# Raw loads of q and k queued quarter by quarter, and the first pair's second-head masks put later

## The chip, the cores and the metric

The kernel runs on one core of a Trainium2 chip. The metric is the device time of one execution in microseconds (us), the median of several runs. TensorE (PE) does the matrix products, VectorE (DVE), ScalarE (ACT) and GpSimd (POOL) the elementwise work, and SyncE (SP) issues nearly all DMAs, one after another, on one queue.

## The reference

Three layers follow each other. The first is attention in clusters: every query and every key is assigned to one of 16 centroids of its head, and a query sees only the keys of its own cluster. Two layers over 1536 tokens come behind it: a dense one with a SiLU, and one that sends each token to one of eight experts.

```python
q_assign = np.argmax(np.einsum('bhsd,hcd->bhsc', q_n, c_n), axis=-1)
k_assign = np.argmax(np.einsum('bhsd,hcd->bhsc', k_n, c_n), axis=-1)
mask = q_assign[:, :, :, None] == k_assign[:, :, None, :]
scores = np.where(mask, scale * np.matmul(q, k.transpose(0, 1, 3, 2)), -1e9)
attn = softmax(scores) ; out = np.matmul(attn, v)      # B, H, S, D = 2, 8, 768, 64
x = out as [1536, 512] ; h = x @ w_in ; x = (h * sigmoid(h)) @ w_out
logits = x @ w_gate + modality_bias[modality_id] ; e = argmax(logits)
out = max(softmax(logits)) * (relu(x @ w1[e]) @ w2[e])
```

## The kernel before

Attention works on eight pairs of heads, one pair after another. For each pair the raw q, k and v come from memory (`load`), are turned into operands for the score product (`prep`), and then run through twelve chunks of 128 queries (`chunk_ops`).

The operands of a pair lie in one tile `opn`, of which there are two, `opn_0` for even pairs and `opn_1` for odd ones. It has four parts, QQ, K1, QX and KX. A score product of a chunk is two kinds of matmul: QQ by K1 (L578), and QX by KX (L581), both added in a bank `big`; there are two such banks. Three steps lead to the operands:

- **Raw loads.** v is one DMA of 384 KB (L347). q and k of pair 0 are two DMAs each (L351). q and k of the later pairs are loaded blocked, in four DMAs each, one for a quarter of the partitions (L356), and DVE transposes them in blocks of 32 (L411).
- **Moves.** ACT and POOL write halves of QQ, K1, KX and a tile `lq`; SP copies them into the other halves of the partitions (L474).
- **Masks.** A chain of seven steps on DVE and PE (L488 to L508) finds every query's and key's cluster and leaves it in `clu_0oq`; POOL makes `clu_0ok` of it (L514). For pair 0 ACT and DVE copy both into rows 64 to 95 of QX and KX (L542, L546), four copies each: two heads by two halves of the tokens. For the other pairs four DMAs do that (L538): two from `clu_0oq` into QX, two from `clu_0ok` into KX.

Then each chunk has its score product, its row maximum on DVE (`nm`, L600), its exponential on ACT (`p`, L606), six transposes on PE (`t`, L617) with their copies to `pt` on ACT (L202) or DVE (L205); every third chunk also sends the reciprocals of its row sums through memory (`rsc` L667, `rb` L672), and a product with v follows (L680). Pair 0 runs head 0 for six chunks, then head 1. Beside it the weights of the later layers begin to be loaded, the gate weights, modality ids and biases (L822 to L825) among them.

No order is written out. Every piece of work is an `op` with a guessed duration, a priority (`prio`, a lower number goes first), the pieces it depends on and the tiles it takes, and `Sched.run` plays them through, at each step taking for each engine the best that can start. What it finds is the order of the instructions on each engine; each engine then runs its own list strictly in order. One `op` may hold several instructions: before the change a blocked load of q or k is one `op` with four DMAs that stand together. `soft` lets a piece start behind the start of what it depends on, not behind its end, `hold` lets an engine wait a little for a piece of better priority, and `port` marks work of DVE that the planner doesn't put beside POOL's.

Of the kernel before, what the change touches and what calls it, by code (L numbers as in the profile page):

```python
# [24 lines left out]
class Sched:  # L25
# [21 lines left out]
    def op(self, eng, dur, fn, deps=(), uses=(), alloc=(), prio=0.0, lat=None, name="", soft=False, eager=False, xfer=None, hold=False, port=False):  # L47
        o = Op()

        o.alts = [a if len(a) == 4 else (*a, port or a[0] == "Pool") for a in (eng if isinstance(eng, list) else [(eng, dur, fn)])]  # L50
        o.prio, o.end, o.n = prio, None, len(self.ops)
        o.deps = [d for d in deps if d is not None]
        o.uses, o.alloc = list(uses), list(alloc)
        o.lat = lat
        o.name, o.soft, o.eager, o.xfer, o.hold = name, soft, eager, xfer, hold
        for u in o.uses:
            u.left += 1
        self.ops.append(o)
        return o
# [128 lines left out]
P = 128  # L188
B, H, S, D = 2, 8, 768, 64
NPAIR = B * H // 2  # L190
NC6 = S // P
# [37 lines left out]
def attention(tc, sc, pools, q, k, v, centroids, ident, xT, opts):  # L229
    nc = tc.nc  # L230
    if True:
# [5 lines left out]
        def sbt(buf, shape, dt=F32, part=""):  # L237
            return pools["a_early" if buf.tag in EARLY else "a_sb"].tile(shape, dt, tag=buf.key + part, name=buf.key + part)
# [7 lines left out]
        op = sc.op  # L246
# [29 lines left out]
        o_h = op("Pool", 300, hmask, prio=-96)  # L276
# [15 lines left out]
        o = op("DVE", 400, cnorm1, deps=[o_cl], prio=-90)  # L292
        o = op("Act", 100, lambda: nc.scalar.activation(cn, css, AF.Sqrt), deps=[o], prio=-90)
        o = o_norm = op("DVE", 1900, cnorm2, deps=[o], prio=-90)
# [19 lines left out]
        o = op("PE", 213, ctr, deps=[o, o_id], uses=[mbc], alloc=[mbc], prio=-90)  # L314
# [9 lines left out]
        for f in (lambda: nc.vector.tensor_scalar(pcol, pcol, 4, None, ALU.logical_shift_right),  # L324
# [8 lines left out]
            o_h = op("DVE", 100, f, deps=[o_h, o_norm], prio=-20, lat=None)  # L333

        raws, ops, Sops, xops, wait = {}, {}, {}, {}, []

        def load(p):
            b, hp = divmod(p, H // 2)
            r = raws[p] = {}
            base = 12.0 * (p - 1) - 12  # L340
            for n, (nm, src) in enumerate((("q", q), ("k", k), ("v", v))):
                buf = Buf("raw" + nm)

                def f(nm=nm, src=src, buf=buf):
                    if nm == "v":
                        buf.tile = sbt(buf, [P, 2, NC6, D])
                        nc.sync.dma_start(buf.tile, src[b, 2 * hp:2 * hp + 2].rearrange("h (c p) d -> p h c d", c=NC6))  # L347
                    elif p == 0:
                        buf.tile = sbt(buf, [P, NC6, 2 * D])
                        for h in range(2):  # L350
                            nc.sync.dma_start(buf.tile[:, :, h * D:(h + 1) * D], src[b, 2 * hp + h].rearrange("(c p) d -> p c d", c=NC6))  # L351
                    else:
                        buf.tile = sbt(buf, [P, S // 32, 32])
                        for a in range(4):
                            half = slice(32 * (a % 2), 32 * (a % 2) + 32)
                            nc.sync.dma_start(buf.tile[32 * a:32 * a + 32], src[b, 2 * hp + a // 2].rearrange("(g j) d -> j g d", j=32)[:, :, half])  # L356
                o = op("SP", 475 if nm == "v" else 1900 if p else 900, f, deps=[raws[p - 1][nm][1]] if p > 1 or p and nm == "v" else [], uses=[buf], alloc=[buf], prio=base + 0.1 * n + (opts.get("v0", 11.5) if nm == "v" and p == 0 else 0), xfer=2400 if nm != "v" and p else 1800)
                r[nm] = (buf, o)
                if p == 1 and nm != "v":
                    o.prio = -23.0 + 0.1 * n  # L360
                elif p == 0 and nm == "v" or p == 2:
                    wait.append(o)

        def prep(p):

            base = 12.0 * (p - 1)
            hp = p % (H // 2)
            pb = opts.get("pb", -1)

            def op(eng, dur, fn, deps=(), uses=(), alloc=(), prio=0.0, lat=None, name="", gated=False, xfer=None, hold=False, port=False):  # L370

                gate = Sops.get(int(prio)) if p > opts.get("g1", 1) and gated else None
                return sc.op(eng, dur, fn, deps=list(deps) + [gate], uses=uses, alloc=alloc, prio=prio + (pb[eng if isinstance(eng, str) else eng[0][0]] if isinstance(pb, dict) else pb), lat=lat, name=name or f"prep{p}", xfer=xfer, hold=hold, port=port)
            buf, lq = Buf("opn"), Buf("lq")
# [11 lines left out]
            evs, his, los, lo1 = [], {}, {}, []  # L386
# [70 lines left out]
            scores = op("PE", 734 if p else 903, fsc, deps=[o for _, o in evs] + [o_cT], uses=[mb] + [fb for fb, _ in evs], alloc=[mb], prio=base + 4.2, gated=True)  # L457
# [7 lines left out]
            for dst, src, h, r, hs, rs, deps in (("K1", "K1", 0, L_, 0, T, halves(his, "k")), ("QX", "QQ", 0, T, 0, T, halves(his, "q")),  # L465
# [6 lines left out]
                def f(dst=dst, src=src, h=h, r=r, hs=hs, rs=rs):  # L472
                    s = tl["lq"].bitcast(F32)[rs] if src == "lq" else tl[src].bitcast(F32)[rs, hs]
                    nc.sync.dma_start(tl[dst].bitcast(F32)[r, h], s)  # L474
                moves.append(op("SP", 650, f, deps=deps, uses=[buf] + ([lq] if src == "lq" else []),
                                prio=base + (4 if p else -20) + 0.01 * len(moves), xfer=546))
# [4 lines left out]
            cb = Buf("clu")  # L481
# [35 lines left out]
            o = scores  # L517
            cl = []
            steps = [dve(c0), dve(c1), dve(c2), dve(c3), [("PE", 163, c4)], dve(c5)]
            for n, a in enumerate(steps):  # L520
                o = op(a, 0, None, deps=[o], uses=[cb] + ([mb] if n in (0, 4, 5) else []), alloc=[cb] if n == 0 else [],
                       prio=base + (5 + 0.1 * n if p else 0.1 * n), hold=not p, port=n == 2 and p > 0)
                cl.append(o)
            okops = []
            for h in range(2 if p else 0):
                okops.append(op([("Pool", 481, lambda h=h: c7(h)("Pool"))], 0, None,
                                deps=[o, o_h], uses=[cb], prio=base + 6))
            mops, mq = [], []
# [12 lines left out]
            def fmq(x, h):  # L541
                nc.scalar.copy(tl["QX"][MR, h, x * HALF:(x + 1) * HALF], ct["oq"][64 * x:64 * x + 32])  # L542

            def fmk(x, h):
                r = slice(64 * x + 32, 64 * x + 64)
                nc.vector.tensor_scalar(tl["KX"][MR, h, x * HALF:(x + 1) * HALF], ct["oq"][r], hrow[r, h:h + 1], hneg[r, h:h + 1], ALU.mult, ALU.add)  # L546
            if p == 0:

                xops["masks"] = cl[-1]

                op("Act", 1300, lambda: nc.scalar.activation(ct_, ct_, AF.Exp), deps=list(los.values()) + [o_norm], prio=base + 5)
                for h in range(2):
                    for x in range(2):
                        mq.append(op("Act", 415, lambda x=x, h=h: fmq(x, h), deps=[cl[-1]], uses=[cb, buf], prio=base + 0.8 + h))
                        mops.append(op("DVE", 480, lambda x=x, h=h: fmk(x, h), deps=[cl[-1], scores, o_h], uses=[cb, buf], prio=base + 0.8 + h, hold=h == 0))
            for ti in range(2 if p else 0):
                for x in range(2):
                    mops.append(op("SP", 650, fm(x, ti), deps=(okops + [scores, moves[3]] if ti else [cl[-1]]),
                                   uses=[cb, buf], prio=base + 6, xfer=273))
# [139 lines left out]
        for p in range(npairs):  # L699
            load(p)  # L700
            if p == 2:
                for o in wait[1:]:
                    o.deps.append(xops["moved"])
            prep(p)
            both = {}

            for x, h in ((0, 0), (1, 0), (0, 1), (1, 1)) if p == 0 else ((0, 0), (0, 1), (1, 0), (1, 1)):
                grp = {}
                for c in range(3 * x, 3 * x + 3):
                    chunk_ops(p, h, c, i, grp, both)  # L710
                    i += 1
# [958 lines left out]
```

## Time and profile before

| | us |
|---|---|
| median of 3 runs (717.13 to 719.17) | 717.97 |
| the profiled execution | 723.03 |
| its span from first to last instruction | 721.2 |
| TensorE busy in the span | 695.5 (96%) |
| VectorE, ScalarE, GpSimd busy | 505.9, 415.3, 127.3 |

The profiled execution is 1.83 us longer than its span and 5.06 us longer than the median. Attention fills about the first 230 us. Start times below count from the start of the span. In a row of a timeline, the brackets at the end give the idle time of the engine ahead of that instruction and what ended it; SPq rows are issues of DMAs, and their duration is that of the issue, not of the transfer.

### The profile page before, as it was taken

The numbers are of one execution on the slowest core, as the hardware profiler recorded it, in microseconds if no ns is written. First come the engines' busy times: TensorE is split into PE (matmuls) and PEld (weight loads), VectorE is DVE, ScalarE is ACT, GpSimd is POOL, SyncE is SP. The second block draws the span as 40 slices with busy tenths as digits, with TensorE's granted clock in tenths as the row PEclk, the third lists the DMA queues.
The fourth block names the chain that finished last, engine by engine and source line by source line (L and its number), as shares of the span: only waits on it lengthen the run. The fifth ranks groups of instructions, "written<-read, shape, count | busy, mean of one in ns | idle before, by whom it ended". The sixth has DMA issues, their size and how long they took to land. (4 is left out here: it accounts for less than half of the span.)

```text
span 721.2 us, 11749 instructions
## 1 busy us (share of the span) xinstructions
PE 695.5 (96%) x4098; PEld 557.6 (77%) x4098; DVE 505.9 (70%) x977; ACT 415.3 (58%) x747; POOL 127.3 (18%) x164
## 2 busy tenths in 40 slices
PE   7989999999999999999999999999998998999995
PEld 6856776776777799999988999999786766877663
DVE  7867988887885789887487444433897885699530
ACT  4855776776776555554343334322737886868631
POOL 6431431431300000000013000000134113222011
PEclk9999999999999999999999999999999999999999
DMA  9865866843520676775016721000115679544850
GB/s 189 155 131 112 179 132 151 169 103 66 132 76 18 201 252 224 250 234 187 30 44 213 294 65 59 29 1 1 51 40 176 208 273 363 180 148 159 271 220 27
DMA packets 104338, 104.82 MB, mean 145 GB/s; under 512 B 70668, under 2 KB 75024, under 8 KB 104272
## 3 DMA queue, kind: packets, MB, share of 16 engines
q1 hardware_dynamic: 101728, 96.56, 46.2%
q0 software_dynamic: 2400, 7.41, 2.9%
q8 instruction: 34, 0.56, 0.3%
q14 instruction: 32, 0.26, 0.1%
q10 hardware_dynamic: 144, 0.03, 0.0%
HBM read 104.99 MB, written 15.17 MB: 167 GB/s over the span
## 5 line engine op out<-in xcount | busy, mean ns | idle before, releaser
L1283 PE MATMUL bank<-whl,whl 128*128 128x384 f32 x768 | 145.7, 338 | 1.0 <-DVE whl L200 0.6
L1283 PEld LDWEIGHTS bank<-whl,whl 128*128 128x128 f32 x768 | 135.5, 188 | 6.9 <-DVE whl L200 1.0
L200 DVE TENSOR_TENSOR whl<-w,whl 128x1024 fp32r<-128x1024 f32 (+2 forms) x100 | 113.1, 1164 | 11.5 <-ACT whl L202 11.1
L600 DVE TENSOR_REDUCE nm<-big 128x1 f32<-128x768 f32 x96 | 90.5, 951 | 25.6 <-PE big L581 24.3
L202 ACT ACTIVATE whl<-w 128x1024 fp32r<-128x1024 f32 (+2 forms) x96 | 95.5, 1028 | 19.7 <-PE bank L1410 9.2
L606 ACT ACTIVATE p<-big,nm 128x768 f32<-128x768 f32 x96 | 86.7, 903 | 33.5 <-DVE nm L600 33.4
L617 PEld LDWEIGHTS t<-ident,p 128*128 128x128 f32 x576 | 67.5, 142 | 15.0 <-issue 9.0
L617 PE MATMUL t<-ident,p 128*128 128x128 f32 x576 | 78.5, 277 | 0.0
L1410 PE MATMUL bank<-whl,xb 128*128 128x512 f32 x288 | 78.0, 416 | 0.5 <-ACT xb L1393 0.5
L1452 PE MATMUL bank<-whl,w 128*128 128x512 f32 x288 | 74.3, 400 | 0.0
L202 ACT ACTIVATE pt<-t 128x384 f32<-128x384 f32 x121 | 55.5, 494 | 30.5 <-PE t L617 30.1
L680 PE MATMUL t<-pt,rawv 128*64 128x384 f32 x384 | 68.9, 494 | 0.0
L1410 PEld LDWEIGHTS bank<-whl,xb 128*128 128x128 f32 x288 | 54.2, 196 | 15.7 <-issue 2.8
L1452 PEld LDWEIGHTS bank<-whl,w 128*128 128x128 f32 x288 | 52.3, 188 | 11.6 <-issue 1.2
L1060 POOL TENSOR_SCALAR row<-L,mx 128x8 f32<-128x8 f32 x12 | 4.8, 400 | 274.4 <-PE bank L1027 148.8
L680 PEld LDWEIGHTS t<-pt,rawv 128*64 128x64 f32 x384 | 25.0, 136 | 30.1 <-issue 28.4
L200 DVE TENSOR_TENSOR whl<-wraw,whl 128x1024 fp32r<-128x1024 f32 x31 | 37.8, 1223 | 14.6 <-ACT whl L202 14.6
L202 ACT ACTIVATE whl<-wraw 128x1024 fp32r<-128x1024 f32 x31 | 32.5, 1056 | 25.5 <-DVE wraw L921 21.7
L578 PE MATMUL big<-opn_0K,opn_0QQ 128*128 128x384 f32 x96 | 37.1, 390 | 3.0 <-ACT p L606 2.6
L205 DVE COPY pt<-t 128x384 f32<-128x384 f32 x71 | 38.5, 543 | 1.1 <-PE t L617 0.3
L1324 PE MATMUL bank<-whl,g_0w 128*128 128x512 f32 x144 | 38.4, 393 | 0.0
L1324 PE MATMUL bank<-whl,g_1w 128*128 128x512 f32 x144 | 37.6, 393 | 0.3 <-DVE g_1w L200 0.3
(311 smaller groups left out, 1099.7 us busy)
## 6 DMA issues: line engine op xcount, KB each, us to landing
w<-in_moe_w_dram SPq DMA_DIRECT2D x88, 512.0 KB
w<-in_moe_w_out_dram SPq DMA_DIRECT2D x8, 1024.0 KB
wraw<-wsc SPq DMA_DIRECT2D x16, 512.0 KB
wsc<-wraw SPq DMA_DIRECT2D x15, 512.0 KB
w<-in_moe_w_in_dram SPq DMA_DIRECT2D x7, 1024.0 KB
wraw<-in_moe_w_dram SPq DMA_DIRECT2D x8, 512.0 KB
x2d<-row SPq DMA_DIRECT2D x12, 260.0 KB
rawv<-in_v_dram SPq DMA_DIRECT2D x8, 384.0 KB
```

The lines of the kernel that those rows point to most:

```text
L200: (nc.vector if e == "DVE" else nc.gpsimd).tensor_tensor(dst, a, b, op)
L202: nc.scalar.activation(dst, a, AF.Copy, scale=1.0 if scale is None else scale)
L205: nc.vector.tensor_copy(dst, a)
L578: nc.tensor.matmul(sb.tile[:, x, :HALF], t["QQ"][:, h, cs], t["K1"][:, h, sl(x)], start=True, stop=False)
L600: nc.vector.tensor_reduce(nb.tile, sb.tile[:, :, :HALF], AX.XY, ALU.max, negate=True)
L606: nc.scalar.activation(pb.tile.rearrange("p (a b) -> p a b", a=2), sb.tile[:, :, :HALF], AF.Exp, bias=nb.tile[:, 0:1], scale=1.0, accum_ou ...
L617: nc.tensor.transpose(tbs[x].tile[:, j * P:(j + 1) * P], pb.tile[:, kc * P:(kc + 1) * P], ident)
L680: nc.tensor.matmul(yb.tile[rows[z], :HALF], raws[p]["v"][0].tile[:, z, kc], w["grp"][z]["tile"][:, kc], start=(kc == 0), stop=(kc == NC6 - 1))
L1283: nc.tensor.matmul(hb.tile[:, :HALF], w[:, ws, dc, fs], xx[:, s, cs], start=(dc == 0 and n == 0), stop=(dc == 3 and n == 2))
L1324: nc.tensor.matmul(ab.tile, gb.tile[gs][:, js], w[:, ws, fc % 2], start=(fc == 0 and n == 0), stop=(fc == 15 and n == 2))
L1410: nc.tensor.matmul(hbs[x].tile, xs_[:, s, dc], w.tile[:, ws, x * 512:(x + 1) * 512], start=(dc == 0 and n == 0), stop=(dc == 3 and n == 2))
L1452: nc.tensor.matmul(ob.tile, hT.tile[:, s, fc * P:(fc + 1) * P], w.tile[:, ws, i * 512:(i + 1) * 512], start=(fc == 0 and n == 0), stop=(fc ...
```

## The change

Three things change, all in what the planner is told; no computation changes, and no instruction is new but one more piece of bookkeeping.

- A blocked load of q or k is now four `op`s with one DMA each, that follow one another softly, so other work of SP can stand between them. For pairs 2 to 7 the priority of the raw loads is 5 later. The two halves of pair 0's loads are `op`s of their own too.
- The mask copies of pair 0's second head have a priority that is 13 later than before, and those on DVE are marked `port`.
- Two pieces on POOL, the low parts of K for pair 0's second head (`lo1`), wait for the two mask copies of its first head on DVE.

```diff
-                def f(nm=nm, src=src, buf=buf):
+                def whole(src=src, buf=buf):
+                def head(h, src=src, buf=buf):
+                def quarter(a, src=src, buf=buf):
...
-                o = op("SP", 475 if nm == "v" else 1900 if p else 900, f, deps=[raws[p - 1][nm][1]] if p > 1 or p and nm == "v" else [], uses=[buf], alloc=[buf], prio=base + 0.1 * n + (opts.get("v0", 11.5) if nm == "v" and p == 0 else 0), xfer=2400 if nm != "v" and p else 1800)
+                fs = [whole] if nm == "v" else [lambda h=h, f=head: f(h) for h in range(2)] if p == 0 else [lambda a=a, f=quarter: f(a) for a in range(4)]
+                pr = base + 0.1 * n + (opts.get("rawp", 5.0) if p > 1 else 0)
...
+                for k_, f in enumerate(fs):
+                    o = op("SP", 475 if p == 0 else 620, f, deps=[o] if k_ else deps, uses=[buf], alloc=[] if k_ else [buf], prio=pr, soft=k_ > 0,
+                           xfer=1800 if nm == "v" else 900 if p == 0 else 640)
...
-                        mq.append(op("Act", 415, lambda x=x, h=h: fmq(x, h), deps=[cl[-1]], uses=[cb, buf], prio=base + 0.8 + h))
-                        mops.append(op("DVE", 480, lambda x=x, h=h: fmk(x, h), deps=[cl[-1], scores, o_h], uses=[cb, buf], prio=base + 0.8 + h, hold=h == 0))
+                        mq.append(op("Act", 415, lambda x=x, h=h: fmq(x, h), deps=[cl[-1]], uses=[cb, buf], prio=base + 0.8 + 14 * h))
+                        mops.append(op("DVE", 480, lambda x=x, h=h: fmk(x, h), deps=[cl[-1], scores, o_h], uses=[cb, buf], prio=base + 0.8 + 14 * h, hold=h == 0, port=True))
+                for o in lo1:
+                    o.deps.extend(mops[:2])
```

What stands in the programs as built, at three places. First SP in pair 0, ahead of pair 1's mask copies (the QX and KX copies from `clu_0oq` and `clu_0ok`); `rawq` and `rawk` here are the loads of pairs 2 and 3. Before:

```order
L822 DMA wg<-in_moe_w_gate_dram 128x4x8
L824 DMA mids<-in_moe_modality_id_dram 128x12x2
L825 DMA bias_114<-in_moe_modality_bias_dram 128x16
L474 DMA opn_1K_382<-opn_1K_382 64x768
L474 DMA opn_1QQ<-lq_385 64x768
L474 DMA opn_1KX<-opn_1KX 64x768
L474 DMA opn_1K_382<-opn_1K_382 64x768
L474 DMA opn_1QQ<-lq_385 64x768
L356 DMA rawq_519<-in_q_dram 32x24x32 x4
L356 DMA rawk_551<-in_k_dram 32x24x32 x4
L538 DMA opn_1QX<-clu_0oq 32x2x384 x2
L538 DMA opn_1KX<-clu_0ok 32x2x384 x2
```

Now:

```order
L485 DMA opn_1KX<-opn_1KX 64x768
L485 DMA opn_1K_378<-opn_1K_378 64x768
L357 DMA rawk_383<-in_k_dram 32x24x32
L357 DMA rawq_505<-in_q_dram 32x24x32 x4
L835 DMA wg<-in_moe_w_gate_dram 128x4x8
L837 DMA mids<-in_moe_modality_id_dram 128x12x2
L838 DMA bias_114<-in_moe_modality_bias_dram 128x16
L357 DMA rawk_572<-in_k_dram 32x24x32
L549 DMA opn_1QX<-clu_0oq 32x2x384 x2
L549 DMA opn_1KX<-clu_0ok 32x2x384 x2
L680 DMA rsc<-rr_441 128x2x3
L357 DMA rawk_572<-in_k_dram 32x24x32 x3
```

Three quarters of pair 3's k stand behind the mask copies now; the gate weights, ids and biases have come down from ahead of pair 1's moves to behind them.

Second, DVE from the start of pair 0's row maxima (`nm`) to the cluster chain of pair 1 (`clu_0s` is its first step). Before:

```order
L508 SCALAR_TENSOR_TENSOR clu_0oq<-t_282,clu_0t 128x384
L546 TENSOR_SCALAR opn_0KX<-clu_0oq,hrow,hneg 32x384 x4
L600 TENSOR_REDUCE nm_351<-big_337 128x1
L600 TENSOR_REDUCE nm_360<-big_346 128x1
L411 STREAM_TRANSPOSE full_365<-rawq_215 128x384
L411 STREAM_TRANSPOSE full_374<-rawq_215 128x384
L411 STREAM_TRANSPOSE full_387<-rawk_229 128x384
L600 TENSOR_REDUCE nm_393<-big_369 128x1
L205 COPY pt_400<-t_395 128x3x128
L600 TENSOR_REDUCE nm_419<-big_402 128x1
L488 STREAM_TRANSPOSE clu_0s<-t_409 128x384
```

Now its first rows, and after those left out (...) the rows from the fifth maximum on:

```order
L422 STREAM_TRANSPOSE full_327<-rawk_233 128x384
L557 TENSOR_SCALAR opn_0KX<-clu_0oq,hrow,hneg 32x384 x3
L613 TENSOR_REDUCE nm_353<-big_337 128x1
L613 TENSOR_REDUCE nm_358<-big_341 128x1
...
L613 TENSOR_REDUCE nm_449<-big_429 128x1
L205 COPY pt_397<-t_452 128x3x128
L557 TENSOR_SCALAR opn_0KX<-clu_0oq,hrow,hneg 32x384
L613 TENSOR_REDUCE nm_478<-big_458 128x1
L499 STREAM_TRANSPOSE clu_0s<-t_391 128x384
```

A transpose of pair 1's k came ahead of the masks, one mask copy went behind the fifth maximum, and pair 1's cluster chain starts behind the sixth maximum, not behind the fourth; its last step, `clu_0oq`, stands behind the ninth and not behind the eighth.

Third, SP ahead of pair 4's mask copies. Before:

```order
L474 DMA opn_0K_1378<-opn_0K_1378 64x768
L667 DMA rsc<-rr_1476 128x2x3
L538 DMA opn_0QX<-clu_0oq 32x2x384 x2
L347 DMA rawv_1586<-in_v_dram 128x12x64
L538 DMA opn_0KX<-clu_0ok 32x2x384 x2
L672 DMA rb_1612<-rsc 64x384 x2
```

Now:

```order
L485 DMA opn_0K_1378<-opn_0K_1378 64x768
L357 DMA rawk_1479<-in_k_dram 32x24x32 x2
L680 DMA rsc<-rr_1476 128x2x3
L685 DMA rb_1565<-rsc 64x384 x2
L549 DMA opn_0QX<-clu_0oq 32x2x384
L346 DMA rawv_1588<-in_v_dram 128x12x64
L549 DMA opn_0QX<-clu_0oq 32x2x384
L549 DMA opn_0KX<-clu_0ok 32x2x384 x2
```

The `rb` loads, which wait until `rsc` has been written, have come ahead of the mask copies. The same happens in pairs 2 and 5; in pairs 6 and 7 they stood that way before.

## Rows read from the trace of the kernel before

**Rows 1.** Waits of PE, 0 to 40 and 40 to 80: total us, times, longest.

```profile
PE big L578 <- ACT p L606: 2.4, 2, 1.9
...
PE big L581 <- DMA opn_1KX<-clu_0ok: 2.2, 2, 1.5
```

**Rows 2.** Windows: length, busy us of PE, PEld, DVE, ACT, POOL, then PEclk, DMA share, GB/s.

```profile
18.00:21.40 3.40, 3.30 (x12) 3.21 (x13) 2.71 (x5) 1.90 (x5) 2.62 (x3) 0.50 0.77 117
...
41.90:45.30 3.40, 3.05 (x11) 2.75 (x11) 2.03 (x3) 1.30 (x4) 0.00 (x0) 0.50 0.04 9
...
60.00:220.00 160.00, 159.76 (x1060) 116.08 (x1059) 133.69 (x235) 114.43 (x253) 42.50 (x58) 1.00 0.53 120
```

**Rows 3.** Timeline of PE at the start of pair 1: start us, duration us, instruction.

```profile
38.99 0.45 PE L578 MATMUL big<-opn_1K,opn_1QQ 128*128 128x384 f32 x1
...
40.94 0.41 PE L581 MATMUL big<-opn_1KX,opn_1QX 96*128 96x384 f32 x1 [1.50 <-DMA opn_1KX<-clu_0ok]
...
42.25 0.66 PE L581 MATMUL big<-opn_1KX,opn_1QX 96*128 96x384 f32 x1 [0.72 <-DMA opn_1KX<-clu_0ok]
```

**Rows 4.** Timeline of SP's issues, 24 to 40.

```profile
24.88 3.10 SPq L825 DMA_DIRECT2D bias<-n_moe_modality_bias_dram  x1
...
31.29 3.09 SPq L356 DMA_DIRECT2D rawq<-in_q_dram  x4
34.48 2.55 SPq L356 DMA_DIRECT2D rawk<-in_k_dram  x4
37.13 1.47 SPq L538 DMA_DIRECT2D opn_1QX<-clu_0oq  x2
38.70 1.22 SPq L538 DMA_DIRECT2D opn_1KX<-clu_0ok  x2
```

**Rows 5.** Timeline of DVE and POOL at the end of pair 1's cluster chain.

```profile
30.02 0.53 DVE L508 SCALAR_TENSOR_TENSOR clu_0oq<-t,clu_0t 128x384 f32<-128x384 f32 x1
30.88 0.96 DVE L600 TENSOR_REDUCE nm<-big 128x1 f32<-128x768 f32 x1 [0.33 <-PE big L581]
...
30.66 1.31 POOL L514 TENSOR_SCALAR clu_0ok<-clu_0oq,hrow,hneg 128x384 f32<-128x384 f32 x2 [2.33 <-DVE clu_0oq L508]
```

**Rows 6.** Timelines of ACT, SP, DVE and PE from 6 to 19.

```profile
6.52 0.84 ACT L202 ACTIVATE opn_0QQ<-full 128x768 fp32r<-128x768 f32 x1 [0.16 <-DVE full L207]
7.89 0.49 ACT L202 ACTIVATE full<-t 128x384 f32<-128x384 f32 x1 [0.53 <-PE t L407]
...
8.84 1.19 SPq L474 DMA_DIRECT2D opn_0QX<-opn_0QQ  x2
...
13.02 3.01 DVE L546 TENSOR_SCALAR opn_0KX<-clu_0oq,hrow,hneg 32x384 fp32r<-32x384 f32 x4
16.06 1.82 DVE L600 TENSOR_REDUCE nm<-big 128x1 f32<-128x768 f32 x2
...
14.51 0.59 PE L578 MATMUL big<-opn_0K,opn_0QQ 128*128 128x384 f32 x2 [0.34 <-POOL opn_0KX L200]
...
15.64 0.52 PE L581 MATMUL big<-opn_0KX,opn_0QX 96*128 96x384 f32 x2
18.10 0.69 PE L578 MATMUL big<-opn_0K,opn_0QQ 128*128 128x384 f32 x1 [1.94 <-ACT p L606]
```

**Rows 7.** Windows, as in rows 2, around SP's issue at 24.88.

```profile
27.20:28.20 1.00, 1.00 (x10) 0.97 (x9) 1.00 (x3) 0.93 (x3) 0.13 (x1) 1.00 0.22 10
```

**Rows 8.** Timelines of SP in pairs 4 and 6, and of PE at pair 4's first use.

```profile
111.76 0.54 SPq L667 DMA_DIRECT2D rsc<-rr  x1
...
162.74 0.37 SPq L667 DMA_DIRECT2D rsc<-rr  x1
166.02 1.10 SPq L672 DMA_DIRECT2D rb<-rsc  x2
...
169.67 1.23 SPq L538 DMA_DIRECT2D opn_0KX<-clu_0ok  x2
...
122.69 0.34 PE L581 MATMUL big<-opn_0KX,opn_0QX 96*128 96x384 f32 x1
```

More of the change, by code (lines that the diff above doesn't have):

```diff
@@ L342, in load @@
                 buf = Buf("raw" + nm)
-                def f(nm=nm, src=src, buf=buf):
[L345 to L348, printed above, removed]
+                def whole(src=src, buf=buf):
+                    buf.tile = sbt(buf, [P, 2, NC6, D])
+                    nc.sync.dma_start(buf.tile, src[b, 2 * hp:2 * hp + 2].rearrange("h (c p) d -> p h c d", c=NC6))
@@ L349, in f @@
+                def head(h, src=src, buf=buf):
+                    if h == 0:
                         buf.tile = sbt(buf, [P, NC6, 2 * D])
-                        for h in range(2):
-                            nc.sync.dma_start(buf.tile[:, :, h * D:(h + 1) * D], src[b, 2 * hp + h].rearrange("(c p) d -> p c d", c=NC6))
-                    else:
+                    nc.sync.dma_start(buf.tile[:, :, h * D:(h + 1) * D], src[b, 2 * hp + h].rearrange("(c p) d -> p c d", c=NC6))
+                def quarter(a, src=src, buf=buf):
+                    if a == 0:
@@ L353, in f @@
                         buf.tile = sbt(buf, [P, S // 32, 32])
-                        for a in range(4):
-                            half = slice(32 * (a % 2), 32 * (a % 2) + 32)
-                            nc.sync.dma_start(buf.tile[32 * a:32 * a + 32], src[b, 2 * hp + a // 2].rearrange("(g j) d -> j g d", j=32)[:, :, half])
-                o = op("SP", 475 if nm == "v" else 1900 if p else 900, f, deps=[raws[p - 1][nm][1]] if p > 1 or p and nm == "v" else [], uses=[buf], alloc=[buf], prio=base + 0.1 * n + (opts.get("v0", 11.5) if nm == "v" and p == 0 else 0), xfer=2400 if nm != "v" and p else 1800)
+                    half = slice(32 * (a % 2), 32 * (a % 2) + 32)
@@ new lines, in quarter @@
+                    nc.sync.dma_start(buf.tile[32 * a:32 * a + 32], src[b, 2 * hp + a // 2].rearrange("(g j) d -> j g d", j=32)[:, :, half])
+                fs = [whole] if nm == "v" else [lambda h=h, f=head: f(h) for h in range(2)] if p == 0 else [lambda a=a, f=quarter: f(a) for a in range(4)]
+                pr = base + 0.1 * n + (opts.get("rawp", 5.0) if p > 1 else 0)
+                if p == 0 and nm == "v":
+                    pr += opts.get("v0", 11.5)
+                elif p == 1 and nm != "v":
+                    pr = -23.0 + 0.1 * n
@@ L358, in load @@
+                deps = [raws[p - 1][nm][1]] if p > 1 or p and nm == "v" else []
+                o = None
+                for k_, f in enumerate(fs):
+                    o = op("SP", 475 if p == 0 else 620, f, deps=[o] if k_ else deps, uses=[buf], alloc=[] if k_ else [buf], prio=pr, soft=k_ > 0,
+                           xfer=1800 if nm == "v" else 900 if p == 0 else 640)
+                    if k_ == 0:
+                        start = o
                 r[nm] = (buf, o)
[L359 to L362, printed above, removed]
+                if p == 0 and nm == "v" or p == 2:
+                    wait.append(start)
```

## The prediction, made before the changed kernel was run

> **What bounds the kernel now.** I read the waits of PE first. Ahead of 40 us PE waited for ACT's exponentials, 2.4 us in two waits; between 40 and 80 us it waited for the mask copies into `opn_1KX`, 2.2 us in two waits [rows 1]. Then the windows: from 60 to 220 us PE is busy 159.76 of 160.00 us, so in the rest of attention nothing but PE's own work counts, and time won ahead of 60 us stays won as long as no later wait opens [rows 2]. [...] Last the timeline of SP: the mask copies of pair 1 are issued at 37.13 and 38.70, behind eight quarters of pair 3's q and k that take 3.09 and 2.55 us to issue [rows 4], although `clu_0oq` is done at 30.55 and `clu_0ok` at 31.97 [rows 5]. So at the seam from pair 0 to pair 1 the queue of SP is what PE waits for.
>
> **The change, part by part.** The sum is made on the profiled execution (723.03) and carried over to the median, 717.97, which lies 5.06 lower, as a difference.
>
> *The wait at pair 1.* PE starts the first product at 38.99 and is through with it at 39.44, then stands 1.50 and, a half product later, 0.72 us [rows 3]: 2.22 us. Three of the eight quarters now come behind the mask copies. At 2.55 / 4 = 0.64 us each that is 1.9 us of SP, so the copies go out at 37.13 - 1.9 = 35.2, and at about 35.7 with the later start of pair 0 worked out below. The last one is then issued by 35.7 + (39.92 - 37.13) = 38.5. Before, PE was released 42.25 - 39.92 = 2.33 us behind the end of that issue [rows 3, 4], so now at 40.8. PE itself comes to that half product at 39.44 + 0.35 (the 40.94 product less its overlap, an estimate) + 0.6 for the later pair 0, some 40.4 to 40.6. The wait left over is 0.2 to 0.4; it could be nothing if the stall of 3.10 us at the biases [rows 4] doesn't come back, and 1.0 if it grows. I take 0.2, as the DMAs were nearly idle (share 0.22) in the last microsecond of that stall [rows 7], which makes a gain there about as likely as a loss.
>
> *Is the data ready then?* `clu_0oq` of pair 1 now follows the ninth maximum. That one ended at 31.84 [rows 5]; with 0.53 for the step and 0.6 for the shift it is ready at 33.0, and `clu_0ok`, 1.31 us on POOL, at 34.4. Both lie ahead of 35.7, so this delay of some 2.4 us is hidden by SP's queue; 1.3 us of it would show if SP came earlier.
>
> *The half clock at 41.9.* If PE no longer stands there, its 3.05 us of work run at full clock: 1.5 us won [rows 2].
>
> *The start of pair 0.* ACT now makes both copies of k (0.49 each) ahead of its part of QQ (0.84) [rows 6]. With the first copy at about 7.5, QQ is ready at 7.5 + 2 x 0.49 + 0.84 = 9.3, not at 7.36; SP issued the QX move at 8.84 and can now at 9.35. So the moves, and the first product at 14.51, come 0.5 later. The two products took 14.51 to 16.16; their order is now both first halves, then both second halves, so the first maximum can start when three quarters are through, at 15.0 + 0.75 x 1.65 = 16.25 plus the lag of a product to its maximum, some 16.4. Before it started at 16.06, held by the four mask copies (3.01 us) [rows 6]. Three copies and a transpose now stand there and end at about 15.9, so they hide behind the products. The fourth copy, 0.75 us, moves between the fifth and the sixth maximum. Upper bound for pair 0: 0.4 + 0.75 = 1.2 later. Lower bound: 0.5 earlier, if the stretch at half clock from 18.0 (3.30 us of work) goes as well, since PE's wait ahead of it shrinks by about 0.4. Waits of PE for ACT sit in between and can take some of it. I take 0.6 later. POOL's two pieces for the second head wait for masks but are needed only in chunk 6: nothing.
>
> *The later seams.* In pairs 2, 4 and 5 the `rb` loads, which wait for `rsc`, come ahead of the masks. Pair 6 has that order already: `rsc` issued by 163.11, `rb` at 166.02 (2.91 later), last KX copy by 170.90 (4.88 later) [rows 8]. Put on pair 4: 112.30 + 2.91 + 4.88 = 120.1, and PE uses KX at 122.69 [rows 8]: 2.6 us, against the 2.33 of pair 1. That is 0 by pair 1's row and up to 1.0 if the load of v, which goes ahead of them, holds the copies back. In pairs 2 and 5 fewer quarters stand ahead of `rsc`. I take 0.2 in all.
>
> Other moves (one copy of `pt` from DVE to ACT, the conversions of the dense layer's weights near 200 us) stay on engines that PE doesn't wait for by more than 0.3 us at a time: nothing.
>
> Sum: - 2.2 - 1.5 + 0.2 + 0.6 + 0.2 = **- 2.7 us**: 723.03 becomes 720.3, and the median 717.97 becomes **715.3**.
>
> **Rivals.**
>
> *The clock gives nothing back.* The fall at 41.9 is one execution's, and the timed runs are others. If in most of them the clock does not fall there, the 1.5 is not there to be won: 2.2 - 1.0 = 1.2, so 716.8. For it: PE stood only 1.50 and 0.72 us. Against it: the other fall, at 18.0, followed a wait of about the same size. [...]
>
> *The wait stays.* The biases now stand directly behind four quarters and ahead of the masks. If SP is held 0.8 us longer there than I count, PE waits 1.0 and the clock falls as before: - 2.2 + 1.0 + 0.6 + 0.2 = - 0.4, so 717.6. For it: the 3.10 us for one small DMA [rows 4]. Against it: the 1.9 us taken out are certain. [...]
>
> *Slower: the masks of pairs 2, 4 and 5 come late.* The place is SP ahead of them, where `rb` now waits 2.91 us for `rsc` in front of the masks. It decides when pair 4's last KX copy lands more than 2.6 us behind its issue. At a price of 1.7 in pair 4 (if the v load's transfer adds 2 us), 1.0 each in pairs 2 and 5, and one more stretch at half clock (1.5), that is 5.2, against - 2.9 from the rest: + 2.3, so 720.3. Against it: pair 6 runs in this order, and PE never waits between 60 and 220 us by more than 0.3 [rows 2].
>
> *More.* The stretch at half clock from 18.0 goes too: 1.6 more, 713.7.
>
> **How the numbers follow.** Forecast 0.48, clock 0.16, wait stays 0.18, slower 0.10, more 0.08. About 0.3%, 2.15 us, is what a measurement of this kernel can tell from no change: 715.8 and 720.1 are the bounds. The forecast's own spread is 714.3 to 716.7, of which 0.35 lies below 715.8; with 0.08 from the last case and 0.02 from the clock's, faster has 0.45. Slower has 0.06 from its case and 0.02 from the upper end of the wait: 0.08. The rest, 0.47, is the same. The range for 8 in 10 leaves out most of the slower case and half of the last: 713.4 to 719.0.
>
> **What would show it.** Right: PE's waits for `opn_1KX` between 38 and 45 fall below 0.4 us in all; the granted clock is full from 40 on; pair 1's last KX copy is issued by about 38.5; PE reaches pair 4's KX (122.69 before) some 2.5 to 3 us earlier. Wrong: waits of PE for `opn_0KX` or `opn_1KX` at the seams to pairs 2, 4 or 5, or a first product of pair 0 later than 15.2, or SP held at the biases beyond 35.

## The result, and the profile after

The changed kernel takes 721.8 us (median of 6 runs, 719.01 to 723.74) against 717.5 us of the kernel before on the same chip. The ratio is 1.0063, with a 95% interval of 1.0034 to 1.0091: 4.3 us or 0.6% slower. The forecast was 715.3, 2.7 us faster. Two later executions that ran at a much lower granted clock, one of the run e8 (970.7 us, clock 0.655) and one of the kernel before (1135.2 us, clock 0.557), are left out of all ratios.

The two profiled executions are nearly equally long (spans 720.6 after, 721.2 before), because the stretch behind 540 us took 4.9 us longer in the one of before (last section). So I followed one event through both traces, the start of each score product on PE, as time after minus time before. Up to the first product of the dense layer, which starts at 241.21 after and at 236.87 before, that difference grows to 4.34 us. It stays as it is until 540 us. That it equals the timed difference is partly luck. The last column has the same steps in the run e5 of the next section, the changed kernel with another PSUM bank for the dense layer: there they add up to 1.46. The bank accounts for the handover; of the rest, most is at pair 2, where the clock fell to 0.50 after and stayed at 1.00 in e5.

| stretch | step of the shift, us | shift then, us | step in e5, us |
|---|---|---|---|
| pair 0, to the first product of pair 1 (39.59, was 38.99) | + 0.60 | + 0.60 | + 0.80 |
| seam to pair 1 (third product: 43.95, was 47.49) | - 4.14 | - 3.54 | - 4.15 |
| rest of pair 1 (fifth product: 48.89, was 50.83) | + 1.60 | - 1.94 | + 1.54 |
| seam to pair 2 (third product: 75.30, was 73.38) | + 3.87 | + 1.93 | + 2.31 |
| pairs 2 to 6 (almost all at pair 4's seam) | + 0.22 | + 2.15 | + 0.26 |
| pair 7 | + 1.37 | + 3.52 | + 0.70 |
| handover to the dense layer | + 0.82 | + 4.34 | 0.00 |

The waits of PE after, from 0 to 40 and from 40 to 80 us (in total, times, longest):

```profile
PE big L591 <- ACT p L619: 2.2, 3, 1.7
...
PE big L594 <- DMA opn_0KX<-clu_0ok: 1.6, 1, 1.6
PE big L591 <- ACT p L619: 1.4, 1, 1.4
```

The wait for `opn_1KX` [rows 1] is gone, and two others have come: one for ACT in pair 1, and one for `opn_0KX`, the masks of pair 2. The windows after, with the columns of [rows 2]:

```profile
20.00:23.40 3.40, 3.40 (x19) 2.65 (x12) 1.36 (x3) 2.58 (x6) 3.40 (x4) 0.50 0.80 156
...
41.90:45.30 3.40, 3.40 (x21) 2.08 (x20) 2.39 (x5) 3.40 (x7) 2.16 (x3) 1.00 0.44 87
...
71.20:74.60 3.40, 3.40 (x12) 0.98 (x8) 2.33 (x5) 1.84 (x3) 1.04 (x2) 0.50 0.30 80
60.00:220.00 160.00, 156.92 (x1024) 112.55 (x1023) 130.29 (x231) 111.79 (x246) 42.20 (x58) 0.99 0.54 120
```

The stretch at the lower clock (0.50) is no longer at 41.9; it stands at 71.2, behind the new wait. From 60 to 220 us PE is busy 156.92 us, where it was 159.76. SP's issues of pair 1 after, which answer to [rows 4]:

```profile
33.55 0.71 SPq L838 DMA_DIRECT2D bias<-n_moe_modality_bias_dram  x1
34.31 0.43 SPq L357 DMA_DIRECT2D rawk<-in_k_dram  x1
34.84 1.40 SPq L549 DMA_DIRECT2D opn_1QX<-clu_0oq  x2
36.33 1.24 SPq L549 DMA_DIRECT2D opn_1KX<-clu_0ok  x2
...
38.25 1.62 SPq L357 DMA_DIRECT2D rawk<-in_k_dram  x3
41.37 2.56 SPq L685 DMA_DIRECT2D rb<-rsc  x2
```

The masks are issued by 37.57, earlier than the 38.5 that I expected. But the three quarters that no longer stand ahead of the masks stand ahead of `rb`, whose issue ends at 43.93. DVE takes its work in order and comes to the normalization that needs `rb`:

```profile
46.20 0.68 DVE L698 TENSOR_TENSOR w<-t,rb 128x384 f32<-128x384 f32 x1 [1.91 <-DMA rb<-rsc]
```

It stands there for 1.91 us, with the next maximum behind it; ACT waits for the maximum and PE for ACT: the 1.4 us among the waits. The largest loss is at pair 2's seam. SP before, in that place:

```profile
58.57 1.33 SPq L538 DMA_DIRECT2D opn_0QX<-clu_0oq  x2
60.00 0.59 SPq L538 DMA_DIRECT2D opn_0KX<-clu_0ok  x1
60.68 0.54 SPq L347 DMA_DIRECT2D rawv<-in_v_dram  x1
61.27 0.77 SPq L538 DMA_DIRECT2D opn_0KX<-clu_0ok  x1
62.09 1.23 SPq L672 DMA_DIRECT2D rb<-rsc  x2
```

and after:

```profile
56.97 0.95 SPq L680 DMA_DIRECT2D rsc<-rr  x1
57.96 1.04 SPq L357 DMA_DIRECT2D rawk<-in_k_dram  x2
61.82 1.11 SPq L685 DMA_DIRECT2D rb<-rsc  x2
63.03 0.90 SPq L549 DMA_DIRECT2D opn_0QX<-clu_0oq  x1
64.03 0.53 SPq L346 DMA_DIRECT2D rawv<-in_v_dram  x1
64.61 0.81 SPq L549 DMA_DIRECT2D opn_0QX<-clu_0oq  x1
65.47 1.23 SPq L549 DMA_DIRECT2D opn_0KX<-clu_0ok  x2
```

SP is idle from 59.00 to 61.82 because `rb` waits until `rsc` is written (it lands at 61.76), and all the mask copies stand behind it. The last one is issued by 66.70 instead of 62.04, while PE comes there 1.9 us earlier than before. PE in the timeline after:

```profile
69.15 0.41 PE L594 MATMUL big<-opn_0KX,opn_0QX 96*128 96x384 f32 x1 [1.60 <-DMA opn_0KX<-clu_0ok]
```

In pair 7 it is DVE again. The timeline of DVE after, and then that of before in the same place:

```profile
200.97 0.95 DVE L613 TENSOR_REDUCE nm<-big 128x1 f32<-128x768 f32 x1
203.92 0.56 DVE L205 CAST whl<-w 128x768 fp32r<-128x768 f32 x1 [2.00 <-DMA opn_1KX<-clu_0ok]
204.39 0.95 DVE L613 TENSOR_REDUCE nm<-big 128x1 f32<-128x768 f32 x1
```

```profile
199.12 0.95 DVE L600 TENSOR_REDUCE nm<-big 128x1 f32<-128x768 f32 x1
199.98 0.55 DVE L205 COPY pt<-t 128x384 f32<-128x384 f32 x1
200.62 0.96 DVE L600 TENSOR_REDUCE nm<-big 128x1 f32<-128x768 f32 x1
...
202.83 0.55 DVE L205 CAST whl<-w 128x768 fp32r<-128x768 f32 x1
```

The conversion `whl<-w` of a dense weight waits for pair 7's mask copies. I take it that it writes where `clu`, which they read, has lain; `whl` and `clu` are in pools that follow each other on the same side of memory; no run tests this by itself. Before, a maximum and a copy stood ahead of it and it found the copies done. Now it is called up earlier, and a maximum stands behind it.

At the handover, last, PE after and DVE after:

```profile
241.21 0.44 PE L1296 MATMUL bank<-whl,whl 128*128 128x384 f32 x1 [0.75 <-DVE w L698]
```

```profile
240.50 0.66 DVE L698 TENSOR_TENSOR w<-t,rb 128x384 f32<-128x384 f32 x1 [4.44 <-PE t L693]
```

Before, the product started ahead of the normalization, so PE did not wait for it:

```profile
236.87 0.44 PE L1283 MATMUL bank<-whl,whl 128*128 128x384 f32 x1
```

```profile
236.98 0.67 DVE L685 TENSOR_TENSOR w<-t,rb 128x384 f32<-128x384 f32 x1 [4.43 <-PE t L680]
```

### The profile page after: what moved, and what is told of

It reads as the page before. It is cut to its first block, busy times and chain, and to the rows that moved or that the text cites. A ratio compares the mean times of both kernels' runs of the same rounds, so it can differ in the third digit from the quotient of the medians.

```text
span 720.6 us, 11757 instructions
## 1 busy us (share of the span) xinstructions
PE 695.7 (97%) x4098; PEld 556.7 (77%) x4098; DVE 505.3 (70%) x976; ACT 415.7 (58%) x748; POOL 123.8 (17%) x164
## 5 line engine op out<-in xcount | busy, mean ns | idle before, releaser
L1423 PE MATMUL bank<-whl,xb 128*128 128x512 f32 x288 | 75.9, 408 | 0.0
L693 PE MATMUL t<-pt,rawv 128*64 128x384 f32 x384 | 70.6, 504 | 0.0
L591 PE MATMUL big<-opn_1K,opn_1QQ 128*128 128x384 f32 x96 | 36.8, 383 | 2.8 <-ACT p L619 2.8
```

Source lines behind the costliest of these rows:

```text
L591: nc.tensor.matmul(sb.tile[:, x, :HALF], t["QQ"][:, h, cs], t["K1"][:, h, sl(x)], start=True, stop=False)
L693: nc.tensor.matmul(yb.tile[rows[z], :HALF], raws[p]["v"][0].tile[:, z, kc], w["grp"][z]["tile"][:, kc], start=(kc == 0), stop=(kc == NC6 - 1))
L1423: nc.tensor.matmul(hbs[x].tile, xs_[:, s, dc], w.tile[:, ws, x * 512:(x + 1) * 512], start=(dc == 0 and n == 0), stop=(dc == 3 and n == 2))
```

## The experiments

All but the one on the PSUM bank alone are replays: the kernel's order on every engine is kept word for word as a table, and only the named instructions move. The other instructions' orders can't shift with them. Ratios are to the kernel before on the same chip, with 95% intervals. They were made in four sessions, in which the kernel before took 717.5 (e1 to e4), 721.6 (e5 to e7), 721.2 (e8 to e11) and 721.8 us (e12).

**Pair 2's masks ahead of `rb`** (e1). SP at pair 2's seam:

```diff
 rawk x2
-rb x2
 opn_0QX, rawv, opn_0QX, opn_0KX x2
+rb x2
```

> The changed kernel in its own order on every engine, but for one thing: at pair 2's seam SP issues the two rb loads (which wait until rsc has landed) behind the four mask copies and the rawv load instead of ahead of them. Theory 1 (the loss in pair 2 comes from that order): KX's two copies are issued 3 to 5 us earlier, PE's wait of 1.60 us for opn_0KX at 69.15 is gone and with it the 3.4 us at half clock that follow at 71.2, PE reaches pair 3 some 3.3 to 3.9 us earlier than in the changed kernel, and the time falls from 721.8 to 718 to 718.6. Rival (the quarters as such crowd the queues, and the copies land late in whatever order): PE still waits over 1 us for opn_0KX and the time stays at 721.3 to 722.3. Second rival (the gain is taken back by pair 7 and the start of the dense layer): the wait is gone but the time falls by under 1.5.

Ratio 1.0030 [1.0013, 1.0046], 2.4 us less than the changed kernel's 1.0063 by the ratios. The one wait of PE over 1 us from 38 to 80 us, and SP's issues:

```profile
PE big L591 <- ACT p L619: 1.4, 1, 1.4
```

```profile
58.92 0.49 SPq L346 DMA_DIRECT2D rawv<-in_v_dram  x1
59.47 2.04 SPq L549 DMA_DIRECT2D opn_0QX<-clu_0oq  x1
61.59 1.23 SPq L549 DMA_DIRECT2D opn_0KX<-clu_0ok  x2
```

The last copy is issued by 62.82 instead of 66.70 and the wait is gone: theory 1 holds. The gain is smaller than the 3.2 to 3.8 expected, though the intervals do not exclude these. One reason may be that 1.70 of the 3.87 is half clock, which does not come in every execution (below). In this one it came in pair 1 instead, from 48.11, behind the 1.4 us above: the shift goes from -2.69 at the fifth product to -1.15 at the seventh, and stays there through pair 2's seam.

**Pair 1's `rb` ahead of the last three quarters** (e2).

```diff
 rsc
-rawk x3
 rb x2
+rawk x3
```

> The changed kernel in its own order on every engine, but for one thing: in pair 1 the last three of the four rawk quarters are issued behind the two rb loads of pair 0, where they stood ahead of them. Theory 2 (DVE, which takes its work in order, stands at the normalization w because these rb loads are late): DVE's wait of 1.91 us for rb at 46.20 falls under 0.5, PE's wait of 1.40 for the exponentials near 47 falls with it, and score product S16 starts 1.2 to 1.6 earlier than in the changed kernel. Since pair 2's wait for its masks is untouched and ends by SP's order, most of that is given back there: time 720.8 to 721.8. Rival (the rb loads are slow by themselves, 2.56 us to issue): DVE still waits over 1.5 us at w and S16 does not move.

Ratio 1.0082 [1.0063, 1.0102]. DVE's wait for `rb` and PE's for ACT are gone, and PE is 3.13 us ahead of before at the fifth product, not 1.94. Of these 1.19 us 0.64 are lost 20 us later, where PE waits longer for the same masks, and the rest by pair 4's seam:

```profile
PE big L594 <- DMA opn_0KX<-clu_0ok: 2.6, 1, 2.6
```

So theory 2 holds for the place and brings nothing at the end.

**The order of before from pair 7 on** (e3). DVE around the conversion:

```diff
-nm, CAST whl<-w, nm, pt, pt, whl<-w,whl x4
+nm, pt, nm, whl<-w,whl x4, CAST whl<-w
```

> The changed kernel until pair 7, and from there on every engine the order (and the choice of engine) that the kernel before has; nothing ahead of pair 7 is touched. Theory 3 (2.4 of the 4.3 us are lost in pair 7 and at the handover to the dense layer, where the conversions whl of the first dense weights and the last normalizations stand in another order on DVE and ACT): the shift against the kernel before stays at about 2 us from pair 3 through to the first product of the dense layer, and the time is 719.2 to 720.0. Rival (the shift at the dense layer follows from pair 2's loss alone, the order there is as good as the other): time 721.3 to 722.3.

Ratio 1.0060 [1.0039, 1.0082]: by the time nothing can be told. By the trace pair 7 loses nothing now (the shift is -0.74 ahead of it and behind it), where 1.37 had been lost. The wait of 0.7 us for the last normalization remained, so it comes from something else. Up to pair 6 this execution has the order of the changed kernel, and yet it is 0.74 ahead of before where that one was 2.15 behind. PE's waits from 38 to 80 us and the windows show why:

```profile
PE big L591 <- ACT p L619: 1.4, 1, 1.4
PE big L594 <- DMA opn_0KX<-clu_0ok: 0.9, 1, 0.9
```

```profile
20.00:23.40 3.40, 3.31 (x26) 2.45 (x19) 2.34 (x6) 3.40 (x7) 3.40 (x4) 1.00 0.91 171
68.10:71.50 3.40, 3.40 (x19) 1.91 (x19) 2.60 (x4) 1.25 (x3) 0.00 (x0) 1.00 0.09 30
```

PE stood 1.73 us at 18.49 and 0.9 at pair 2's seam, and the clock fell behind neither: it is 1.00 in both windows.

**Only pair 3's loads behind pair 1's masks, in the kernel before** (e4, and again as e8).

```diff
-rawq x4, rawk x4
 opn_1QX x2, opn_1KX x2, rsc, rsc, rb x2, rb x2
+rawq x4, rawk x4
```

> The kernel before, with its loads unsplit and its whole order kept, but for one thing: pair 3's rawq and rawk issues (two DMA groups of four) stand behind pair 1's four mask copies and behind the rsc and rb of pair 0, instead of ahead of the masks. If the gain at pair 1's seam is only a matter of what stands ahead of the mask copies on SP, and not of the split: PE's waits for opn_1KX (1.50 and 0.72) and the half clock at 41.9 are gone, the seam is 3.4 to 4.5 us earlier, pair 2's masks stay ahead of its rb, and the time is 712.9 to 714.5, below both kernels. Rival (the shift is swallowed in pair 2 or at the dense layer's start): the waits in pair 1 are gone but the time falls by under 1 us, 716.5 to 717.5.

Ratio 0.9978 [0.9959, 0.9997]: 2.0 us less by the medians, between the forecast and its rival. From the first to the third product of pair 1 PE gains 4.15 us, where the changed kernel gained 4.14: what brings the gain there is the order, not the split. Then PE waits for pair 2's masks here too, since it comes 4.2 us earlier and SP has four quarters of `rawk` to issue ahead of them (3.01 us, from 53.33):

```profile
PE big L581 <- DMA opn_0KX<-clu_0ok: 1.3, 1, 1.3
```

Of 4.2 us, 2.6 are left at the dense layer (234.29).

**Another PSUM bank for the dense layer's first tile** (e5).

```diff
 pools.open("m_ps", space=PSUM, reuse_waits="tile")
+pools["m_ps"].tile([P, 512], F32, tag="bank_4", name="bank_4")
```

> The changed kernel with one line added: the dense layer's first PSUM tile (bank_0) gets bank 1 of PSUM instead of bank 0; nothing else moves. In the changed kernel the last attention product (the tile t that the last normalization w reads) lies in PSUM bank 0, and in the kernel before in bank 3. Theory 4: that is why PE waits 0.75 us for DVE's w at the start of the dense layer (241.21) and did not before; then the wait is gone and the first dense product starts 0.7 to 0.8 us earlier relative to the last score product (14.2 us after score product 94 now, 13.4 in the kernel before). Rival (the products need the normalized values themselves): the wait stays at 0.7 to 0.8. The single time decides nothing here: 719 to 724.

One execution was timed, 721.7 us, which decides nothing. The wait is gone, and the product is 13.4 us behind score product 94 (224.92), as in the kernel before. PE and DVE:

```profile
238.33 0.44 PE L1296 MATMUL bank<-whl,whl 128*128 128x384 f32 x1
```

```profile
238.44 0.67 DVE L698 TENSOR_TENSOR w<-t,rb 128x384 f32<-128x384 f32 x1 [4.43 <-PE t L693]
```

Theory 4 holds. Which of the four `t` tiles the last product gets comes out of the planner's times, so an early move can change it: in e10 a move in pair 2 brings the wait of 0.8 us into the kernel before.

**All of it at once** (e6: the edits of e1, e2, e3 and e5), **and pair 2's `rawv` behind the masks as well** (e12).

```diff
-opn_0QX, rawv, opn_0QX, opn_0KX x2, rb x2
+opn_0QX x2, opn_0KX x2, rb x2, rawv
```

> The changed kernel with all that the runs point to put right at once: pair 2's rb behind its mask copies, pair 1's last rawk quarters behind pair 0's rb, the order of before from pair 7 on, and the dense layer's first tile in another PSUM bank. The loads stay split and pair 0's mask edit stays. If the losses are these four and nothing else: PE is 3.1 us ahead of the kernel before at the end of pair 1, waits under 1.2 for pair 2's masks, and starts the dense layer 1.9 to 3.1 us ahead of the kernel before: 714.4 to 715.6. Rival (a part of the loss is in the split loads or in pair 0, unseen so far): 717 or more.

Ratio 1.0017 [0.9996, 1.0037]: better than the changed kernel, but not than before, and the 1.9 to 3.1 us expected did not come. PE still waited 1.8 us for pair 2's masks:

```profile
60.26 0.53 SPq L346 DMA_DIRECT2D rawv<-in_v_dram  x1
60.84 2.15 SPq L549 DMA_DIRECT2D opn_0QX<-clu_0oq  x1
63.08 1.79 SPq L549 DMA_DIRECT2D opn_0KX<-clu_0ok  x2
```

> The kernel of e6 (the changed kernel with its orders put right) with one more move: pair 2's rawv load, which SP issues between the mask copies of pair 2, goes behind them and behind rb. In e6 the mask copies were ahead of rb and PE still waited 1.79 us for them; the copies that stand behind rawv landed within 0.7 us of it (68.62; 68.85, 69.07, 69.30). Theory: the large load holds up the small copies behind it. Then the last mask copy lands some 3 us earlier, by 66.3, PE's wait at pair 2 is gone, PE starts the dense layer 2 to 3 us ahead of the kernel before, and the ratio to the kernel before is 0.995 to 0.998. Rival (the copies are late by their own issue times): the wait stays at 1.3 to 1.8 and the ratio at 1.000 to 1.002.

Ratio 0.9965 [0.9947, 0.9983], below the kernel before. SP:

```profile
59.09 1.33 SPq L549 DMA_DIRECT2D opn_0QX<-clu_0oq  x2
60.52 1.22 SPq L549 DMA_DIRECT2D opn_0KX<-clu_0ok  x2
61.84 1.80 SPq L685 DMA_DIRECT2D rb<-rsc  x2
63.73 0.53 SPq L346 DMA_DIRECT2D rawv<-in_v_dram  x1
```

The last mask copy lands at 65.63, not 69.30, and PE's wait is gone. Of these 3.67 us 3.13 are already in the issues: the last one ends at 61.74, in e6 at 64.87, where the issues behind `rawv` took 2.15 us (one copy) and 1.79 (two). The transfer shows in the kernel before, where pair 2's two copies into KX stand on either side of `rawv`: issued by 60.58 and by 62.04, they landed at 62.24 and at 65.88, and `rawv` at 65.27. So here the load of 384 KB held up the small copy behind it in the queue: 3.84 us from the end of its issue to its landing, against 1.66 for the copy ahead of the load.

**The kernel before with more loads moved** (e7, e10, e11; e8 and e9 beside them): pair 4's `rawk` and pair 2's `rawv` behind pair 2's masks and `rb`, too, with and without the other bank.

```diff
-rawk x4
 opn_0K, opn_0KX, opn_0K, rsc, opn_0QX x2
-opn_0KX, rawv, opn_0KX, rb x2
+opn_0KX x2, rb x2, rawk x4, rawv
```

> The kernel before, loads unsplit, with pair 3's rawq and rawk behind pair 1's masks and pair 0's rb, as in the run on that edit alone, and now pair 4's rawk and pair 2's rawv behind pair 2's masks and pair 1's rb as well, and the dense layer's first tile in another PSUM bank (the new order would have put the last attention product in its bank). If pair 2's masks were late only by what SP issues ahead of them: the wait of 1.32 us for opn_0KX at 66.97 is under 0.3, PE keeps the 4.2 us that it won at pair 1's seam to the start of the dense layer (near 232.7), and the time is 713.0 to 714.2, the fastest of all. Rival (the masks' chain on PE, DVE and POOL sets their time): the wait stays over 1 and the time is that of the other run, 715 to 716.

Ratio 0.9968 [0.9947, 0.9989]. PE had no wait at pair 2 and came to the dense layer at 231.55, 5.3 us ahead of before; the span, 715.5, is 5.7 us shorter than that of before. But by the medians of the timed runs only 1.9 us are won. Four runs on one chip asked why.

> The kernel before with pair 3's rawq and rawk behind pair 1's masks, as in e4, now beside the three runs that follow, on one chip. PE waits some 1.3 us for pair 2's masks and is 2.6 us ahead of the kernel before at the start of the dense layer; ratio to the kernel before 0.996 to 0.998.

> As the run ahead of it, but the dense layer's first PSUM tile is in bank 1 instead of 0. Here the last attention product lies in bank 3, so nothing is to be won. Theory 5 (the gain of the run e7 was given back behind 540 us because the other PSUM banks slow the expert stage): 2 us or more slower than the run ahead of it. Rival (what comes back behind 540 us differs from execution to execution): within 0.8 us of it.

> The kernel before with pair 3's loads behind pair 1's masks, and pair 4's rawk and pair 2's rawv behind pair 2's masks and pair 1's rb, as in e7, without the change of the PSUM bank: the new order puts the last attention product in bank 0, so PE waits 0.75 us for the last normalization at the dense layer's start. No wait for pair 2's masks; PE is 4.2 to 5.3 us ahead at the end of pair 7 and 3.5 to 4.5 at the dense layer's start. If that comes out at the end: ratio 0.993 to 0.995. If the expert stage gives a part back whatever the bank: 0.996 to 0.998, as e7 had.

> The kernel of e7 once more, beside the three others on one chip. By theory 5 (the banks slow the expert stage) it is 1 us or more slower than the run ahead of it; by the rival it is 0.7 us faster, the 0.75 us of wait that the bank takes away: ratio 0.992 to 0.995, or 0.996 to 0.998 if the expert stage gives back a part in any case.

Ratios: e8 0.9971 [0.9953, 0.9990], e9 0.9958 [0.9938, 0.9979], e10 0.9976 [0.9959, 0.9993], e11 0.9958 [0.9942, 0.9974]. Theory 5 falls: with the other bank both are lower, though the intervals overlap. e9 and e11, some 3 us faster than the kernel before, are the best seen. The edit of pair 2 brings nothing that can be measured. In both of its executions here the wait at pair 2 was gone (the shift stays at -3.66 and -3.50), but by pair 4 it had shrunk to -1.23 and -1.58. DVE in e10, and in e7:

```profile
83.45 0.43 DVE L877 TENSOR_SCALAR firstt<-first 128x512 uint32<-128x512 uint32 x1 [3.39 <-DMA first<-in_moe_w_in_dram]
```

```profile
78.78 0.43 DVE L877 TENSOR_SCALAR firstt<-first 128x512 uint32<-128x512 uint32 x1 [0.41 <-DMA first<-in_moe_w_in_dram]
```

DVE and ACT stand 3.4 and 3.5 us in order for the load of `first`, a piece of the dense layer's weights. SP issued it at 76.72, 3.5 us later than in e7 (73.24), though PE was only 1.7 us later than in e7: it stands behind the moved loads and behind one more round trip of `rsc` and `rb`. In e7, with the same order, it was nearly in time. So e7's 5.3 us are one execution's, and nothing of them came back behind 540 us. A part is the clock, which did not fall in its pair 0: at the first product of pair 1 it is 1.00 ahead of before, where the other five with that order (e4, e8 to e11) lie from 0.06 ahead to 0.85 behind. e11, the same kernel as e7, came to the dense layer only 1.59 ahead.

## Why the prediction was wrong, point by point

*The wait at pair 1 and the half clock behind it: right.* Forecast -2.2, +0.2 and -1.5, together -3.5; measured -4.14. The residual wait of 0.2 is none, because the issue of the biases took 0.71 us and not 3.10 again, the case named beside it. By e4 the order of the mask copies does it. The size rests on one trace of the kernel before, in which the clock fell at 41.9; whether it falls there in its other executions no run shows.

*Pair 0: right, and its size partly luck.* Forecast +0.6 and a first product 0.5 later; measured +0.60, and 0.38 later. The first product starts at 14.76 to 15.29 in the seven executions with pair 0's new order, and at 14.14 to 14.60 in the seven without. The shift of pair 1's first product scatters more, from -0.46 to +2.30 with the new order and from -1.00 to +0.85 without: the clock, at 0.50 for 3.4 us in pair 0 of the kernel before, did not fall there in e1, e3, e7 and e12, and fell for twice as long in e6.

*The later seams: the step that failed.* Forecast 0.2 in all, measured 3.87 at pair 2 (2.17 of it around the wait, 1.70 at half clock) and 0.22 at pair 4. "In pairs 2 and 5 fewer quarters stand ahead of `rsc`" was argued from a count. I worked out the slack of pair 4 alone, from pair 6's rows, and took pair 2 to have no less. From the issue of `rsc` to that of `rb` it took 4.85 us in pair 2 (56.97 to 61.82), where pair 6 had 2.91 from the end of the one to the start of the other [rows 8] (3.91 in pair 2, reckoned so). And PE comes to this seam earlier by what was won at pair 1. The rival of late masks had the mechanism and the sign, with the place in pair 4; its price for the wait in pair 2, 1.0, was less than half of what came, and the 1.5 for a stretch at half clock was about right.

*What stands behind the masks: missed.* The forecast counted the three quarters out of the way of the masks and did not ask whom they stand in the way of next. They stand ahead of `rb`: 1.60 us of PE in pair 1. By e2 this costs nothing at the end as long as pair 2's masks are later still.

*"Other moves ... nothing": wrong.* These were 1.37 us in pair 7 (0.70 to 1.37 in the four executions with that order) and 0.82 at the handover. Both are waits that the trace of before does not show, because there the data had always been ready: a conversion that waits for pair 7's mask copies (e3), and a PSUM bank whose last reader is late (e5). The moved rows were to be seen in the order; I priced their durations and not what they wait for.

*The clock.* The rival "the clock gives nothing back" said that the fall at 41.9 is one execution's. That is borne out in another place: behind the wait for pair 2's masks the clock fell in the changed kernel (1.60 us of wait), but not in e5, which has the same order there and waited 1.69:

```profile
69.10:72.50 3.40, 2.98 (x15) 1.77 (x17) 1.94 (x3) 0.89 (x2) 0.00 (x0) 1.00 0.12 28
```

The shift grew by 3.87 there in the changed kernel, by 2.31 in e5 and, without a fall and with 0.9 of wait, by 1.14 in e3. e4 and e8 are one kernel, and at this place the clock stayed up behind 1.3 us of wait in e4 (1.00 from 68.80 to 72.20) and fell behind 1.8 in e8 (0.50 there). So the length of the wait alone did not decide it: the clock fell behind 1.60 us and not behind 1.69. That a wait brings a fall was an estimate from the two falls in one trace [rows 2]; what makes the clock fall no run shows.

*In order.* In e6 and e12 the landings came in the order of the issues: behind `rawv`, which landed at 68.62, the copies landed at 68.85, 69.07 and 69.30 (e6); ahead of it, at 64.68 to 65.63 (e12).

## What to carry to other kernels

An instruction that is put behind another is put ahead of a third: of every move on an in-order queue, list who stands behind its new place, and work out the slack of each of them from its own rows, not from a neighbour's. A load that waits for a round trip through memory does not belong ahead of small copies that PE needs soon: ahead of `rb`, SP stood from 59.00 to 61.82 with the mask copies behind it. Nor does a large load, even when it is issued in half a microsecond: `rawv` was issued in 0.54 us, and the copy behind it landed 3.84 us after its issue, the one ahead 1.66. Time won early can make the next seam the bound, as in e4, where 2.6 of 4.2 us were left, so the slack there has to be reckoned against the earlier arrival.

## What was not expected of the hardware

The same instructions behind 540 us, where the routed experts run, take a different time in each execution. From the first product of the dense layer to one near the end (number 2592 from there) it was 466.1 us in e4, 466.6 in e3, 466.8 after, and 471.4 in e7 and 471.7 before; up to 540 us all of them agree within 0.05 us. It goes with the session: the five executions from where the kernel before takes 717.5 us (after, e1 to e4) lie from 466.1 to 466.8, the eight from where it takes 721.2 to 721.8 from 468.9 to 471.4. Why is open; it is the reason why profiled spans could not be compared here.

An issue on SP does not have one price: the same `rb` pair took 1.11 us at 61.82 and 2.56 at 41.37, and the load of the biases 3.10 before and 0.71 after.
